# A list schedule whose due times come from its own latest times, from the first microsecond and in four passes

## The chip, the cores and the metric

The kernel runs on one core of a Trainium2 chip. The metric is the device time of one execution in microseconds (us). The engines named below are TensorE (PE, with its weight loads PEld), VectorE (DVE), ScalarE (ACT), GpSimd (POOL) and SyncE (SP), whose queue issues nearly all DMAs.

## What is computed

Attention over 4 batches of 8 heads, 768 positions and head size 64, in which a query sees the last 96 positions and the first 8 (with a linear penalty on the distance), followed by a dense layer of width 2048 with an ELU between its two products.

```python
scores = scale * np.matmul(q, k.transpose(0, 1, 3, 2))
scores = np.where(keep, scores + bias, -1000000000.0)
a = np.exp(scores - np.max(scores, axis=-1, keepdims=True))
x = (a / (np.sum(a, axis=-1, keepdims=True) + 1e-09)) @ v     # then heads side by side: (3072, 512)
h = x @ w_in                                                  # (512, 2048), stored as float64
g = np.where(h > 0.0, h, np.exp(np.minimum(h, 0.0)) - 1.0)
return g @ w_out                                              # (2048, 512), stored as float64
```

## The kernel before

The 3072 rows are cut into 12 groups of 256. The weights are cut into 16 chunks (fc 0 to 15) of each matrix. Every fp32 factor is split into a high and a low part, so a product takes three matmuls (high by high, high by low, low by high).

Groups 0 to 2 are computed plainly. Their attention works on pairs of heads (`pair32`, L677): scores on PE (L691), bias and maximum on DVE (L647), exponential on ACT (L649), the reciprocal of the sum on DVE (L662, L663), the scaling on ACT, DVE or POOL (L633, L635, L637), transposes (L708), their copies (tile `pt`), the product with v (L725), and the split of its result into tile `xh`. Their dense layer (`moe`, L737) runs fc 0 to 4 for the three groups, then fc 5 to 9, then 10 to 15: matmuls `h` (L803), the ELU (`elu`, L731: ACT, ACT, DVE), its split into `gh` and `gl`, and two steps later the matmuls `o` (L763). The pairs' loads share three buffers for `rqv` and three for `rk`.

The weights arrive as float64 bits. `weight` (L413) turns each of the 32 chunks into two fp32 parts: a load (L425), one ACT and four DVE operations (L433 to L442), a cast on ACT, a subtraction on POOL or DVE; 24 of the chunks are then stored again in DRAM (`kept`, L449). `combos` (L453) builds sums of second-layer weights, which groups 3 to 11 need: they compute the second product in seven block products instead of eight (`moe7`, L808, matmuls `a`, L877). Group 3's attention is still of the plain kind; those of groups 4 to 11 are woven between the matmuls in `visit` (L596).

No order of work is written by hand. `build` (L930) adds some thousands of operations to a `Plan`, each with the engines that can do it and a cost in ns for each, the tiles that it reads and writes, and a due time worked out by hand: d - 8000 for the ELU, d - 5500 to d - 2000 for a weight's steps, where d is the time at which the chunk's matmuls are meant to run; the start of group 3 plus 6.6 us for each chunk's `combos`; windows in `ATT` for attention. The hand-written start of group 3 is 178.8 us (30.0 + 16 x 3.5 + 32 x 2.9).

`order` (L147) is a list schedule. Of the operations that an engine could start next it takes one that can start now over one that must wait, and among those the one with the earliest due time. Tiles of one class are given buffers in the order in which they were added, whatever is due. An operation with several engines goes to the one that would finish it first, by where those engines stand, not by what is queued for them. PE operations of the late groups have a fixed sequence (`seq`).

`latest` (L115) goes backwards over a finished plan. PE gets an ideal line: from `since` on its operations in their planned sequence without gaps, and before `since` their planned starts. Every other operation gets the latest time by which it must start so that its consumers, and the next user of its buffer, keep theirs. That time becomes its due time:

```python
at = op.start if at is None or op.start < since else at      # L128, PE's ideal line
if op.seq is None and op.eng != "PE" and op.start > since:   # L141
    op.due = op.late
```

`run` (L1039) plans once by hand-written due times, then `PASSES` times takes latest times and plans again, and emits the last plan. Each engine executes its share in that order. Before emission the loads of chunks 2, 3 and 4 (`ASKED`) are moved to just behind the eleventh load of attention. `run` also puts eleven small operations for an input flag (L1093 to L1108) at a fixed number of places behind the last transposes.

Of the kernel before, what the change touches and what calls it, by code (L numbers as in the profile page):

```python
# [275 lines left out]
class Kernel:  # L276
# [732 lines left out]
    PERIOD, SECOND, DOWN, DOWN2, VISIT = 13200.0, 2890.0, 6730.0, 9250.0, 9245.0  # L1009
    OPENS = (0, 2, 6)  # L1010
    AFTER = 2 * PERIOD
    PASSES, SINCE = 2, 195000.0
    GS, KEEP, COMBO = 3, 100000.0, 0.0
    LATE, ASKED = 11, (2, 3, 4)
    ABS = (0, 1)
# [294 lines left out]
```

## Time and profile before

| | us |
|---|---|
| median of 3 runs | 657.53 (656.42 to 657.7) |
| the profiled execution | 657.34 |
| its span, first to last instruction | 655.6 |
| PE, DVE, ACT, POOL busy in the span | 641.5, 521.2, 478.2, 39.5 |

The difference of 1.74 us between the profiled execution's time and its span lies around the program. A matmul's end is modelled in the profile, so PE counts as busy through short waits; the wait of a weight load (PEld) for another engine is the sharper sign that PE had nothing to do.

### The profile page before, as it was taken

To read this page: it belongs to the slowest core of one execution; us is meant where nothing else is said; L and a number is where in the kernel's file an instruction comes from. 1 tells how busy PE (TensorE), PEld (TensorE's weight loads), DVE (VectorE), ACT (ScalarE), POOL (GpSimd) and SP (SyncE) were. 2 spreads that over 40 slices of the span, in tenths; PEclk is the share of its full clock that TensorE was granted. 3 is DMA by queue.
4 is the path that set the end of the run, shared out by engine and by line. 5 is a ranking of instruction groups with operands and counts; after the bars stand their busy time and mean duration, and the time that the engine had idled before them with its cause. 6 is when DMAs were issued, how large, how long until landed. Compare 5 with 4: busy or idle time off the path is not lost.

```text
span 655.6 us, 15992 instructions
## 1 busy us (share of the span) xinstructions
PE 641.5 (98%) x5950; PEld 598.6 (91%) x5950; DVE 521.2 (80%) x1509; ACT 478.2 (73%) x1243; POOL 39.5 (6%) x65
## 2 busy tenths in 40 slices
PE   8899999999999999999999999999999999999996
PEld 6677888888888999999999999999999999999995
DVE  7999999999998867866877886876777778765654
ACT  7998878766878776877777776786777867773542
POOL 4143001110211000000000000000000000000000
PEclk9999999999999999999999999999999999999999
DMA  7936996710237567667766747756775775674751
GB/s 272 307 112 216 389 339 257 264 65 12 77 113 261 185 215 254 221 202 243 241 196 211 267 174 235 250 205 221 227 242 186 248 257 180 210 250 140 248 171 38
DMA packets 52377, 137.75 MB, mean 210 GB/s; under 512 B 5698, under 2 KB 19010, under 8 KB 52290
## 3 DMA queue, kind: packets, MB, share of 16 engines
q1 hardware_dynamic: 52000, 136.37, 61.2%
q8 instruction: 49, 0.80, 0.5%
q10 hardware_dynamic: 290, 0.26, 0.1%
q14 instruction: 38, 0.31, 0.1%
HBM read 119.84 MB, written 16.78 MB: 208 GB/s over the span
## 4 chain that ended last, share of the span: by engine, by line
PE 82%; DVE 12%; ACT 3%; issue 1%; DMA 1%; POOL 0%; POOLq 0%; SPq 0%; DVEq 0%
PE h L803 35%; PE a L877 27%; PE o L763 6%; PE pv L614 4%; PE s L556 3%; PE t L576 3%; DVE g L464 2%; PE pv L725 1%; PE t L708 1%; ACT pr L649 1%; DVE gl L344 1%; DMA rqv<-in_qkv_dram 1%; DVE e L735 1%; PE s L691 1%; DVE g L440 1%
## 5 line engine op out<-in xcount | busy, mean ns | idle before, releaser
L803 PE MATMUL h<-xh,w0s 128*128 128x256 f32 x1728 | 203.1, 276 | 0.0
L803 PEld LDWEIGHTS h<-xh,w0s 128*128 128x128 f32 x1728 | 199.5, 188 | 0.1
L877 PE MATMUL a<-w,gg 128*128 128x256 f32 x864 | 143.7, 277 | 0.3 <-DVE xh L344 0.3
L336 ACT CAST gg<-z 128x384 fp32r<-128x384 f32 (+1 forms) x144 | 81.3, 565 | 70.4 <-DVE z L735 30.4
L735 DVE SCALAR_TENSOR_TENSOR z<-z,h 128x512 f32<-128x512 f32 x72 | 49.5, 688 | 95.2 <-ACT z L734 87.2
L877 PEld LDWEIGHTS a<-w,gg 128*128 128x128 f32 x864 | 120.4, 188 | 0.5 <-DVE xh L344 0.5
L649 ACT ACTIVATE pr<-pr,nmax 128x232 f32<-128x232 f32 (+1 forms) x192 | 90.0, 471 | 9.0 <-DVE nmax L647 8.6
L344 DVE TENSOR_TENSOR gg<-z,gg 128x512 fp32r<-128x512 f32 (+1 forms) x144 | 84.9, 618 | 7.4 <-ACT gg L336 6.6
L803 PEld LDWEIGHTS h<-xh,w 128*128 128x128 f32 x576 | 81.5, 189 | 8.8 <-issue 1.4
L803 PE MATMUL h<-xh,w 128*128 128x256 f32 x576 | 86.9, 283 | 0.0
L835 DVE TENSOR_TENSOR z<-z 128x128 f32<-128x128 f32 (+1 forms) x216 | 72.0, 333 | 5.2
L877 PE MATMUL a<-ta,gg 128*128 128x256 f32 x432 | 72.4, 276 | 0.0
L733 ACT ACTIVATE z<-h 128x512 f32<-128x512 f32 x72 | 43.0, 597 | 34.8 <-PE h L803 34.5
L647 DVE CUSTOM_DVE_ANT_0 pr<-s,tab 128x232 f32<-128x232 f32 (+1 forms) x192 | 63.4, 373 | 5.6 <-PE s L556 5.6
L763 PE MATMUL o<-w,gh 128*128 128x512 f32 x192 | 59.7, 403 | 1.7 <-DVE ob L790 1.2
L877 PEld LDWEIGHTS a<-ta,gg 128*128 128x128 f32 x432 | 59.7, 188 | 0.0
L877 PE MATMUL a<-tb,gg 128*128 128x256 f32 x216 | 50.0, 294 | 0.0
L734 ACT ACTIVATE z<-z 128x512 f32<-128x512 f32 x72 | 45.5, 631 | 1.8
L633 ACT ACTIVATE pr<-pr,st 128x232 f32<-128x232 f32 (+1 forms) x89 | 38.5, 468 | 9.7 <-DVE st L669 7.4
L763 PEld LDWEIGHTS o<-w,gh 128*128 128x128 f32 x192 | 32.0, 188 | 6.8 <-ACT pr L649 1.6
L877 PEld LDWEIGHTS a<-tb,gg 128*128 128x128 f32 x216 | 34.4, 188 | 3.8 <-issue 0.2
L649 ACT ACTIVATION_READ_ACCUMULATOR pr<-pr,nmax 128x1 f32 x192 | 36.8, 191 | 0.0
(128 smaller groups left out, 923.9 us busy)
## 6 DMA issues: line engine op xcount, KB each, us to landing
w0s<-kept SPq DMA_DIRECT2D x144, 512.0 KB, 5.0
rk<-in_qkv_dram SPq DMA_DIRECT2D x45, 184.0 KB, 2.7
bits<-in_w_in_dram SPq DMA_DIRECT2D x16, 512.0 KB, 6.3
bits<-in_w_out_dram SPq DMA_DIRECT2D x16, 512.0 KB, 9.3
kept<-w SPq DMA_DIRECT2D x16, 512.0 KB, 4.4
rv<-in_qkv_dram SPq DMA_DIRECT2D x32, 256.0 KB, 3.6
rqv<-in_qkv_dram SPq DMA_DIRECT2D x13, 384.0 KB, 3.5
rqv<-in_qkv_dram SPq DMA_DIRECT2D x34, 128.0 KB, 3.6
```

Source lines behind the costliest of these rows:

```text
L336: self.nc.scalar.copy(out, x)
L344: self.on(e).tensor_tensor(out, x, y, ALU.subtract)
L633: self.nc.scalar.activation(out, x, AF.Copy, scale=sc)
L647: p.add((("DVE", 158 + 1.042 * n, False),), lambda e: nc.vector.tensor_tensor_reduce(pr.t[:, lo:], st_()[:, lo:], tab, -(2.0 ** -(h + 1)), ...
L649: p.add(act(n, extra=200), lambda e: nc.scalar.activation(pr.t[:, lo:], pr.t[:, lo:], AF.Exp, bias=nm, scale=-1.0, accum_out=st.t[:, 0, i: ...
L733: p.add(act(n, True), lambda e: nc.scalar.activation(out(), hx(), AF.Relu, scale=-1.0), [h], [ex], due)
L734: p.add(act(n), lambda e: nc.scalar.activation(out(), out(), AF.Exp, scale=-1.0), [ex], [ex], due)
L735: p.add(dve(n), lambda e: nc.vector.scalar_tensor_tensor(out(), out(), -1.0, hx(), ALU.add, ALU.max), [h, ex], [ex], due)
L763: nc.tensor.matmul(acc[i].t, g.t[:, i * P:(i + 1) * P], w2.t[:, s], start=fc == f0 and n == 0 and s == HI, stop=fc == f1 - 1 and n == 1)
L803: self.nc.tensor.matmul(hx(), w1.t[:, s, cc * P:(cc + 1) * P], xh.t[:, x, cc], start=n == 0 and cc == 0, stop=n == 2 and cc == self.NCC - 1)
L835: tt = lambda e, out, x, y, op: self.on(e).tensor_tensor(out, x, y, op)
L877: nc.tensor.matmul(of[i].t[:, j], gg.t[:, x, g], w(s), start=first and x == s == 0 and n in (0, 2, 4, 6), stop=last and x == LO and n in ( ...
```

## The change

Two constants of the planner. `SINCE` becomes 0, so that all operations but PE's take their due times from latest times, and PE's ideal line has no gaps from its first operation on; before, that held for what was planned to start after 195 us. `PASSES` becomes 4, so the plan is made five times instead of three. PE's own operations keep the due times and sequence that they had. No operation is added or left out; what can change is the order on each engine, the engine of an operation that has a choice, and the buffer that a tile gets.

```diff
@@ -1009,7 +1009,7 @@
     PERIOD, SECOND, DOWN, DOWN2, VISIT = 13200.0, 2890.0, 6730.0, 9250.0, 9245.0
     OPENS = (0, 2, 6)
     AFTER = 2 * PERIOD
-    PASSES, SINCE = 2, 195000.0
+    PASSES, SINCE = 4, 0.0
     GS, KEEP, COMBO = 3, 100000.0, 0.0
     LATE, ASKED = 11, (2, 3, 4)
     ABS = (0, 1)
```

## Rows read from the trace of the kernel before

**Rows 1.** The profile's page: busy us, share of the span, instructions of each engine.
```profile
PE 641.5 (98%) x5950; PEld 598.6 (91%) x5950; DVE 521.2 (80%) x1509; ACT 478.2 (73%) x1243; POOL 39.5 (6%) x65
```

**Rows 2.** Busy time by stage: stretch, length, engines' busy us (instructions), clock, DMA share, GB/s.
```profile
10.00:60.00 50.00, 45.91 (x370) 35.19 (x371) 48.42 (x166) 45.61 (x145) 15.85 (x24) 1.00 0.62 206
60.00:70.00 10.00, 10.00 (x90) 8.64 (x89) 8.64 (x30) 9.67 (x30) 3.33 (x6) 1.00 1.00 383
70.00:140.00 70.00, 70.00 (x478) 61.32 (x477) 69.14 (x179) 57.24 (x148) 5.48 (x9) 1.00 0.74 274
140.00:200.00 60.00, 58.40 (x409) 50.12 (x408) 59.79 (x150) 41.88 (x119) 9.31 (x10) 1.00 0.24 78
200.00:590.00 390.00, 390.00 (x4049) 379.01 (x4048) 291.21 (x855) 292.22 (x743) 1.55 (x3) 1.00 0.67 224
590.00:606.00 16.00, 15.67 (x148) 15.17 (x148) 9.28 (x27) 6.50 (x12) 0.00 (x0) 1.00 0.41 144
```

**Rows 3.** The chain that ended last, 198 to 590 us, shares by line.
```profile
by line: PE h L803 43.5%; PE a L877 38.3%; PE pv L614 6.8%; PE s L556 5.7%; PE t L576 4.4%; PE o L763 1.1%; PE th L576 0.3%
```

**Rows 4.** The same chain, 590 to 606 us.
```profile
by line: PE h L803 38.3%; PE a L877 18.6%; DVE gg L344 13.3%; DVE z L835 5.9%; DVE z L735 4.3%; ACT z L734 4.0%; DVE xh L344 3.8%; ACT z L733 3.8%; DVE flag L1093 1.7%; issue 1.5%; DVE flag L1100 1.0%; DVE flag L1101 1.0%; DVE flag L1094 1.
```

**Rows 5.** The same chain, 3 to 76 us: shares, then pieces (start, us, what).
```profile
by line: PE o L763 11.8%; ACT pr L649 10.6%; PE pv L725 9.9%; DMA rqv<-in_qkv_dram 9.5%; PE h L803 9.3%; PE t L708 9.3%; PE s L691 6.6%; ACT pt L336 3.8%; issue 3.3%; POOL pr L637 2.8%; DVE gl L344 2.1%; DVE pr L647 2.0%; PE none L1078 1.9%
...
18.98 3.22 DMA rqv<-in_qkv_dram
...
28.86 0.57 ACT g L433
...
45.28 3.74 DMA rqv<-in_qkv_dram
...
54.60 0.60 DVE g L442
```

**Rows 6.** Who waited for whom, 5 to 70 us: total us, times, longest us.
```profile
POOL pr L637 <- DVE st L663: 19.8, 6, 5.4
...
PEld t L708 <- POOL pr L637: 2.7, 7, 0.7
PEld s L691 <- ACT rqv L633: 2.0, 2, 1.7
PEld t L708 <- ACT pt L336: 1.8, 2, 0.9
...
PEld s L691 <- DVE rqv L635: 1.0, 3, 0.6
...
PEld pv L725 <- ACT pr L649: 0.6, 2, 0.4
...
PEld s L691 <- DVE g L440: 0.2, 1, 0.2
```

**Rows 7.** The DMA queue's own waits, 5 to 70 us.
```profile
SPq L516 <- PE pv L725: 20.9, 9, 5.1
```

**Rows 8.** Who waited for whom, 70 to 200 us, PE and its weight loads.
```profile
PE o L763 <- DVE ob L790: 1.2, 1, 1.2
...
PEld o L763 <- ACT pr L649: 1.6, 1, 1.6
PEld o L763 <- ACT gh L336: 0.8, 2, 0.5
PEld o L763 <- DVE gl L344: 0.7, 3, 0.3
```

**Rows 9.** DVE by line, 70 to 140 us: count, busy us, mean ns, idle before.
```profile
L440 DVE SCALAR_TENSOR_TENSOR g<-bits,g 128x512 int32<-128x512 int32 x19 | 12.8, 679 | 0.0
...
L735 DVE SCALAR_TENSOR_TENSOR e<-e,h 128x256 f32<-128x256 f32 x22 | 8.9, 407 | 0.0
L344 DVE TENSOR_TENSOR gl<-e,gh 128x256 fp32r<-128x256 f32 x21 | 8.7, 415 | 0.5 <-ACT gh L336 0.5
```

**Rows 10.** The chain that ended last, 140 to 192 us, shares by line.
```profile
by line: DVE g L464 25.7%; DVE e L735 9.4%; DVE gl L344 8.6%; issue 8.0%; DVE ta L344 7.8%; DVE w L344 4.4%; DVE g L440 4.2%; DVE tb L344 3.6%; PE o L763 3.1%; DVE pr L647 2.9%; PE h L803 2.7%; DVE xh L344 2.7%; DVE ob L790 2.5%; DVE g L442
```

## The prediction

> **What bounds the kernel now.** I read the page first, then the busy time by stage, then the chain that ended last in each stage, and last the waits. The page says PE 98% busy [rows 1], but its busy time is modelled, so the stages matter more. From 200 to 590 us PE is busy without a break, its weight loads for 379.01 of 390 us, while DVE and ACT have 98.8 and 97.8 us to spare [rows 2]; the chain of that stretch is PE alone [rows 3]. There is nothing to win there. Before 200 us it is another kernel: DVE is busy for 48.42 of 50 us, then 8.64 of 10, 69.14 of 70 and 59.79 of 60 [rows 2], because it does attention for groups 0 to 3, the weights' conversion and the `combos`. ACT is nearly as full up to 70 us (45.61 of 50 and 9.67 of 10). From 3 to 76 us only 48.8% of the chain, 35.6 of 73 us, is PE (11.8 + 9.9 + 9.3 + 9.3 + 6.6 + 1.9) [rows 5]; the rest is ACT, DVE, POOL and two loads. So the reader should look for what PE lacks in the first 70 us, and then check that the change doesn't spoil what follows.
>
> What PE lacks there: its weight loads wait 2.7 us for scaled probabilities from POOL, 2.0 and 1.0 us for scaled queries, 1.8 us for copied transposes, and 1.7 us in five smaller rows, the first of 0.6 and the last of 0.2 us [rows 6]: 9.2 us in all. From 70 to 200 us it is 1.6 + 0.8 + 0.7 us and 1.2 us for the output copy `ob`, 4.3 us [rows 8]. These 13.5 us are all that any order of the work could win back before 200 us, and a part of it is owed to engines that are full, not to their order.
>
> **The change, part by part.**
>
> First, no instruction is added or removed. What moves is the order on DVE, ACT, POOL and SP for everything planned before 195 us: softmax, conversion, ELU, `combos`, loads, the `kept` stores. PE's operations keep hand-written due times, and classes of tiles keep their order, so pairs follow pairs and chunks follow chunks as before; what is free is how the streams are interleaved.
>
> Second, from 3 to 76 us. The chain runs through weight conversion that stands ahead of attention on its engine: pieces like 0.57 us of L433 on ACT at 28.86 and 0.60 us of L442 on DVE at 54.60 [rows 5]. POOL shows the same from its side: it sat idle for 19.8 us, six times, waiting for a DVE reciprocal (L663) [rows 6], a step that the plan costs at 0.29 us; its inputs, or it, had queued behind longer work. Hand-written due times can't know which buffer the next pair waits for; latest times do, since they follow the next user of a buffer too. So the short links of the attention chain should get ahead of conversion that PE needs later. What can come of it: the waits on POOL, on `pt` and on small rows (2.7 + 1.8 + 1.7 = 6.2 us) come from order and from capacity together; I take 40%, -2.5 us. The scaled queries (3.0 us) stand behind loads of 3.22 and 3.74 us on the chain [rows 5], which begin as soon as a buffer is free; those I leave. A bound from capacity: between 10 and 70 us DVE is idle for 1.58 + 1.36 = 2.94 us [rows 2]. Work conserved on DVE can't end earlier by more than that unless some of it goes to POOL, which has 40.8 of 60 us free, or to ACT with 4.7. So -2.94 us, and at the far end about -4.5 when a few operations change engine. On the other side, a wrong interleaving can add as much as it can save: +4.5.
>
> Third, from 70 to 200 us. PE is covered now: the ELU's due time of d - 8000 puts it ahead of conversion at d - 5500 and later, and the `o` matmuls come two steps of 2.9 us behind their `h`. The stalls that remain are 1.2 us on `ob`, which the buffer rule of the latest times should see coming, and 1.6 + 0.8 + 0.7 us [rows 8]. With latest times the ELU loses its fixed lead and gets just what the next `o` needs. I book -1.0 us for `ob` and +1.0 us for more stalls of the ELU, together 0; bounds -2 and +5 (the second rival). The `combos` fill a quarter of the chain between 140 and 192 us (25.7% for L464) [rows 10], although group 3's second product is the first to need them; in both kernels they are due last and run only where DVE is free, so they stay where they are, at 0.
>
> Fourth, SP. All loads and `kept` stores get new due times. SP is seldom the one that is late: its longest waits are for buffers (20.9 us in nine waits of L516 for L725 [rows 7]), and an order by need keeps those. Taken at 0; if a conversion load stood ahead of an attention load, the price is what DMA shows on the chain, 3.22 to 3.74 us [rows 5], once.
>
> Fifth, two more passes and a line without gaps. From 200 us on all latest times move earlier by about the same amount, so their order holds, and PE is full in its fixed sequence: 0. One piece can move: the flag's operations and ELU of the last group stand on the chain between 590 and 606 us, where PE's h and a make 56.9% [rows 4]; the flag's place counts operations, so it can slip off or stay: 0, between -1 and +1 us.
>
> Sum: -2.5 (second), 0 (third to fifth). Against the profiled execution's 657.34 us that is 654.8; the median of the runs, 657.53, lies 0.2 us above that execution, so I say 655.0 us, 0.4% faster.
>
> **The rivals.**
>
> Rival A, no change: capacity, not order. DVE and ACT are full where PE waits, so an earlier operation pushes another one back, and PE's own order, which doesn't change, hands the new due times the old interleaving. For it: 48.42 of 50 us on DVE [rows 2]. Against: POOL's 19.8 us behind a reciprocal [rows 6]. It gives 657.5 us, within 1.3 us.
>
> Rival B, slower: the ELU without its lead. From 70 to 140 us DVE has no idle time, and each of the ELU's two DVE steps (0.407 and 0.415 us) can stand behind a conversion step of 0.679 us that began just before [rows 9]. One such step ahead of each costs a chunk 1.4 us, which the 5.8 us between `h` and `o` absorb; three ahead of each (4.1 us) it no longer absorbs together with the chain's own five operations of about 0.4 us (2 us). From there every chunk can stall PE by some 0.3 to 0.7 us. 22 chunks lie between 70 and 140 us [rows 9] and, as an estimate at the same pace, 19 in the 60 us behind them; a quarter of these 41 at 0.45 us is 4.6 us: 662 us. For it: PE's weight loads already wait for gh and gl in five places [rows 8]. Against: the same planner works with latest times after 200 us without a stall; but there DVE is free for a quarter of the time.
>
> Rival C, buffers. Nine times SP waited for the `pv` matmul of an earlier pair before it could load the next queries, 20.9 us in total [rows 7], and the load then stood on the chain. If it is those three buffers that set the pace of attention up to 70 us, any order gives the same stalls, and the time is 657.5 us. The Trainium skill (Perfetto Trace Analysis, Identifying Performance Opportunities) says that the same gap repeated on the engine that should be saturated can mean that there isn't enough memory for the next tile. By that rule the repeated waits of the pairs would be a matter of buffers and my second part would be worth nothing.
>
> Rival D, the plan wanders: each pass plans on the order of the pass before, the last one is taken whether or not it is the best, and the model of the plan is not the chip. Where the first 70 us lose one more load of 3.22 to 3.74 us on the chain [rows 5], the time is 661 us.
>
> The change may also not do what it says where the interleaving is ruled by PE's due times and by the order of the classes; that is rival A.
>
> **How the numbers follow.** Forecast (about 655.0, own range 650.8 to 656.2): 0.43. Rival A 0.15 and rival C 0.10, both at 657.5: 0.25 for no change. Rival B 0.18, rival D 0.14: 0.32 for slower, 659 to 664. A difference of 0.2%, 1.3 us, is about what a measurement of this kernel can tell from no change. The low end is the far bound of the second part with that of the third, -4.5 and -2, 650.8; the high end takes in rival B's 662. Less than 2 in 10 lies outside.
>
> **What would show it.** Right: in the chain from 3 to 76 us fewer pieces of conversion (L433 to L442) and a share of PE above 48.8%; the weight loads' waits for POOL and `pt` below 4.5 us together; group 3's first matmuls `h` of the woven kind some 2 us earlier; from there to the end the same length. Rival A: the same waits in other places. Rival B: waits of `o` for gh and gl between 70 and 200 us well above 1.5 us. Rival C: SP's waits for `pv` near 20.9 us and the attention of group 2 ending where it ended. Rival D: more than two loads of `rqv` on the chain. I am wrong altogether if the stretch after 200 us changes length by over 1 us.

## The result

The changed kernel takes 664.38 us (median of six runs, 663.13 to 665.23) against 657.62 us for the kernel before, measured beside it. The ratio is 1.0091, with a 95% interval of 1.0072 to 1.0109: 0.9% slower, where 0.4% faster was forecast. The profiled execution took 665.16 us, its span is 663.4 us.

The profile's page of the kernel before has these two lines for the matmuls of groups 3 to 11, the first product `h` and one part of the second, `a`:

```profile
L803 PE MATMUL h<-xh,w0s 128*128 128x256 f32 x1728 | 203.1, 276 | 0.0
...
L877 PE MATMUL a<-w,gg 128*128 128x256 f32 x864 | 143.7, 277 | 0.3 <-DVE xh L344 0.3
```

The page of the changed kernel shows more time for the same counts, 4.6 us for `h` and 1.5 us for `a`, of the 8.0 us by which PE's busy time has grown:

```profile
PE 649.5 (98%) x5941; PEld 606.0 (91%) x5941; DVE 519.1 (78%) x1503; ACT 479.9 (72%) x1248; POOL 43.9 (7%) x66
...
L803 PE MATMUL h<-xh,w0s 128*128 128x256 f32 x1728 | 207.7, 279 | 0.0
...
L877 PE MATMUL a<-w,gg 128*128 128x256 f32 x864 | 145.2, 278 | 0.3 <-DVE xh L344 0.3
```

The busy time by stage of the changed kernel, columns as in [rows 2]:

```profile
10.00:60.00 50.00, 45.91 (x362) 34.77 (x362) 46.59 (x159) 45.80 (x146) 14.20 (x23) 0.97 0.56 189
...
70.00:140.00 70.00, 70.00 (x478) 61.22 (x477) 69.38 (x176) 57.05 (x151) 7.82 (x8) 1.00 0.78 294
140.00:200.00 60.00, 59.53 (x417) 51.57 (x417) 59.03 (x154) 43.85 (x123) 15.43 (x16) 1.00 0.24 75
200.00:590.00 390.00, 390.00 (x3985) 379.21 (x3984) 287.34 (x846) 288.06 (x735) 0.78 (x2) 1.00 0.66 220
```

The reader should look at the last line beside that of [rows 2]. PE is full in both, its weight loads are busy for 379 us in both, the clock is 1.00 in both; but in the same 390 us the changed kernel executes 3985 matmuls where the kernel before executed 4049. In this stretch PE waits for nobody, and yet less gets done: its matmuls follow each other more slowly. The stages before 200 us, in which the order of the work changed most, end almost level. (The 9 matmuls fewer on the page, 5941 for 5950, lie there: they are filler matmuls, whose number follows the gaps of the plan, 24 for 22 at L1078 and none for 11 at L1087.) The first woven `h` matmul starts at 202.09 us, before at 201.84 us. From there to the end of the span it is 461.3 us instead of 453.7: 7.6 us, all of the loss.

The chain that ended last shows where. A piece `h x48` is four chunks' worth of matmuls that stream one buffer of tile `xh`. In the kernel before, pieces between 238 and 292 us (start, us, what):

```profile
239.52 5.44 PE h L803 x48
253.16 5.44 PE h L803 x48
264.90 5.44 PE h L803 x48
278.54 5.44 PE h L803 x48
```

In the changed kernel:

```profile
240.05 5.44 PE h L803 x48
253.75 5.74 PE h L803 x48
265.89 5.74 PE h L803 x48
279.91 5.74 PE h L803 x48
```

The first piece belongs to group 3, the others to group 4. Group 3 runs at the old pace, group 4 at 5.74 us, and so it alternates to the end: every second group is slow. Groups alternate between two buffers for `xh`, xh0 and xh1. The slow ones are those on xh1.

So I took the buffer of every PE operation from the two plans and measured in the two traces how far apart the starts of successive matmuls of one operation lie on average (256 columns each; the moving data is streamed through PE, the stationary data is what the weight load puts there):

| matmuls | before | after |
|---|---|---|
| h, moving data in xh0 (960 woven matmuls) | 113.7 ns | 113.9 ns |
| h, moving data in xh1 (768 woven matmuls) | 113.9 ns | 119.6 ns |
| a, stationary data in gg0, moving data in tile `ta` (202 spacings) | 113.7 ns | 117.3 ns |
| a, stationary data in gg1, moving data in `ta` (196) | 113.7 ns | 113.4 ns |
| a, last group, stationary data in xh1 (51) | 113.4 ns | 118.4 ns |
| a, all with stationary data in gg0 (555, some pairs with gaps in both) | 121.0 ns | 123.6 ns |

The built programs say what happened to these buffers. A pool gives addresses in the order in which buffers are first used. In the kernel before, the planned first use of xh1 (group 1's attention result) stood 0.6 us ahead of that of gg0 (the first `gh`). In the changed kernel it stands 0.3 us behind. The two changed places in SBUF, the memory from which PE reads them, and as they differ in size their addresses moved:

| buffer | start before, bytes | by 256 | start after, bytes | by 256 |
|---|---|---|---|---|
| xh0 | 175008 | 160 | 175008 | 160 |
| xh1 | 184736 | 160 | 192224 | 224 |
| gg0 | 193248 | 224 | 184928 | 96 |
| gg1 | 201440 | 224 | 201440 | 224 |
| w012 to w015, the ring of h's weights | 38112, 42208, 8928, 4832 | 224 | the same | 224 |

The constants `PLACE`, with their odd offsets of 32, 48, 80 and 160 words, put these remainders there; they hold only for the order of first use that the old plan gave.

### The profile page after: what moved, and what is told of

It is laid out like the page before. It is cut to its first block, busy times and chain, and to the rows that moved or that the text cites. A ratio compares the mean times of both kernels' runs of the same rounds, so it can differ in the third digit from the quotient of the medians.

```text
span 663.4 us, 15966 instructions
## 1 busy us (share of the span) xinstructions
PE 649.5 (98%) x5941; PEld 606.0 (91%) x5941; DVE 519.1 (78%) x1503; ACT 479.9 (72%) x1248; POOL 43.9 (7%) x66
## 4 chain that ended last, share of the span: by engine, by line
PE 88%; DVE 6%; ACT 2%; issue 1%; DMA 1%; POOL 0%; SPq 0%; POOLq 0%; ACTq 0%
PE h L803 38%; PE a L877 27%; PE o L763 9%; PE pv L614 4%; PE s L556 3%; PE t L576 3%; PE pv L725 1%; PE s L691 1%; PE t L708 1%; DMA bits<-in_w_in_dram 1%; DVE g L440 1%; ACT pr L649 1%; DVE g L442 1%; DVE w L344 0%; DVE g L438 0%
## 5 line engine op out<-in xcount | busy, mean ns | idle before, releaser
L803 PE MATMUL h<-xh,w0s 128*128 128x256 f32 x1728 | 207.7, 279 | 0.0
L803 PEld LDWEIGHTS h<-xh,w0s 128*128 128x128 f32 x1728 | 204.1, 189 | 0.1
L877 PE MATMUL a<-w,gg 128*128 128x256 f32 x864 | 145.2, 278 | 0.3 <-DVE xh L344 0.3
L633 ACT ACTIVATE pr<-pr,st 128x232 f32<-128x232 f32 (+1 forms) x95 | 40.3, 467 | 9.3 <-DVE st L669 7.7
L734 ACT ACTIVATE z<-z 128x512 f32<-128x512 f32 x72 | 45.5, 633 | 1.8
```

The costliest lines, as they stand in the source:

```text
L633: self.nc.scalar.activation(out, x, AF.Copy, scale=sc)
L734: p.add(act(n), lambda e: nc.scalar.activation(out(), out(), AF.Exp, scale=-1.0), [ex], [ex], due)
L803: self.nc.tensor.matmul(hx(), w1.t[:, s, cc * P:(cc + 1) * P], xh.t[:, x, cc], start=n == 0 and cc == 0, stop=n == 2 and cc == self.NCC - 1)
L877: nc.tensor.matmul(of[i].t[:, j], gg.t[:, x, g], w(s), start=first and x == s == 0 and n in (0, 2, 4, 6), stop=last and x == LO and n in ( ...
```

## The experiments

Two theories stood against each other. P: the loss is placement, that is, addresses. S: it is the schedule, in the way of rivals B and D. The first two runs are a cross of the two orders with the two sets of addresses. To hold the addresses, every buffer is touched once in a fixed order before any work; no instruction comes of it.

**Order of the changed kernel, addresses of the kernel before.**

```diff
+    LAYOUT = "w015 w014 w115 w114 ... st5 e1 xh1 gg0 gl0 gg1 gl1 gh2 gl2 qs0 ks0 part0 part1 vd0"
...
         with self.tc.manual_schedule():
+            for s in self.LAYOUT.split():
+                (self.w if s[0] == "w" else self.m).tile([P, self.LINE], F32, tag=s, name=self.n("at"))
             self.setup()
```

> The changed kernel's order of work, but every buffer is given the address that it has in the kernel before (the buffers are touched once, in the old order, before any work). Theory P (placement): the 7 us are lost after 200 us because two buffers, xh1 and gg0, changed places in SBUF, and matmuls that read them take 120 and 117.5 ns instead of 114; with the old addresses h on xh1 is back at 114 ns and the time is 657.6 us, within 1.5. Theory S (schedule: the ELU without its lead, or a wandering plan): the time stays at 664, since the order is that of the changed kernel.

Measured: 657.96 us, a ratio of 0.9997 (0.9988 to 1.0006) to the kernel before. h on xh1 takes 113.9 ns, and the pieces of the chain are back:

```profile
253.21 5.44 PE h L803 x48
264.95 5.44 PE h L803 x48
278.59 5.44 PE h L803 x48
```

The loss is gone although the order on all engines is that of the changed kernel. S falls.

**Order of the kernel before, addresses of the changed kernel.** The same lines, with gg0 ahead of xh1 and the other pairs swapped as the changed kernel has them.

> The order of the kernel before with the addresses of the changed kernel. Theory P: slower by 768 matmuls x 6.1 ns (h on xh1) + 555 x 3.5 ns (a with gg0) + 51 x 5 ns, 6.9 us, so 664.5 us; the first woven h stays at 201.8 us. Theory S: 657.6 us.

Measured: 664.36 us, 1.0097 (1.0081 to 1.0112). h on xh1 takes 119.6 ns, and the chain has the slow pieces:

```profile
252.26 5.74 PE h L803 x48
264.39 5.74 PE h L803 x48
278.42 5.74 PE h L803 x48
```

The addresses alone make the whole loss, on a program whose order wasn't touched. The sum expected was 6.9 us; the medians differ by 6.2.

**SINCE = 0 with two passes, addresses held.**

```diff
-    PASSES, SINCE = 4, 0.0
+    PASSES, SINCE = 2, 0.0
```

> SINCE = 0 with two passes as before, addresses of the kernel before. Theory P: 657.6 us within 1.5, like the changed order on the old addresses. Theory S: near 664, if the due times are to blame and not the further passes. The plan's own end is 0.4 us later than before's, so a schedule effect alone should be under 1 us.

Measured: 655.99 us, 0.9968 (0.9956 to 0.9980). Faster than the kernel before by 2.2 us, more than the bound of 1.5 that I had set. So the new due times can gain something, but not in the plan that four passes arrive at.

**Four passes with SINCE = 195000, addresses held.**

> Four passes with SINCE = 195000, addresses of the kernel before. 50 places of the order differ from the kernel before, and the plan ends at the same time. Both theories: 657.6 us within 1; a change of more would mean that the later groups' order matters by itself.

Measured: 658.38 us, 0.9998 (0.9985 to 1.0011): nothing, as both expected. Two further passes over the late groups only change nothing.

**Which addresses cost.** Four runs of the kernel before, in which xh0 and xh1 are moved inside their room by changing `PLACE` alone, for instance

```diff
-             ... "xh0": (160, 0), "xh1": (32, 0), "gg0": (80, 0), ...
+             ... "xh0": (128, 32), "xh1": (96, 0), "gg0": (16, 0), ...
```

> The kernel before with its two buffers of moving data shifted by some bytes inside their room; everything else stays in place. A start's remainder by 512 bytes was 416 for xh0 and xh1 and 224 for all four weight buffers of the ring; in the changed kernel xh1 had 224. Here xh1 has 160 and xh0 288. If equal remainders are what costs (theory E), both groups of h stay at 114 ns; if only 416 is good (theory G), both go to 120 ns.

> The same with remainders 96 (xh1) and 352 (xh0). Theory E: 114 and 114 ns. Theory G: 120 and 120 ns, about 9.4 us longer in all. A third, that the distance to 224 counts in steps of 64 bytes: between the two.

> The same with remainders 32 (xh1) and 480 (xh0). Theory E: 114 and 114 ns. Theory G: 120 and 120 ns.

> The same with remainders 192 (xh1) and 256 (xh0), 32 bytes to either side of the weights' 224. Theory E with a grain of 64 bytes or more: at least one of the two at 120 ns; with a grain of 32 bytes: both at 114 ns. Theory G: both at 120 ns.

Measured, one run each beside 657.76 us: 662.69, 667.98, 667.54 and 663.84 us. By buffer, the woven h (median over the operations of four matmuls each; the ring's weights stay at 224 by 256):

| start of the moving data by 512 | by 256 | ns |
|---|---|---|
| 160 and 416 | 160 | 113.3 and 113.3 |
| 32 and 288 | 32 | 117.7 and 117.7 |
| 96 and 352 | 96 | 117.3 to 120.3 in both, 118.9 and 119.1 on average |
| 224 and 480 | 224 | 120.0 and 120.0 (the 224 from the changed kernel) |
| 192 | 192 | 117.0 to 119.0 |
| 256 | 0 | 117.0 |

Starts that lie 256 bytes apart give the same spacing, in all four pairs; so for the moving data the address counts by its remainder by 256, as far as these pairs go. Theory E (only equal remainders cost) falls: five of six remainders cost something, equality costs most. G is nearer the truth once it is read by 256, with 160 the only one of the six that costs nothing, though it set all costs at 120 ns. The starts of xh in the kernel before were not neutral ground but the best of the six remainders tried: a move to any other of them loses.

**Is it the distance to the weights?** Three of the ring's four buffers are moved, xh stays.

```diff
-    PLACE = {"w015": (80, 0), "w014": (0, 48), "w012": (80, 0), "w013": (0, 48), ...
+    PLACE = {"w015": (80, 0), "w014": (16, 32), "w012": (64, 16), "w013": (32, 16), ...
```

> The kernel before, with three of the ring's four weight buffers shifted inside their room and the buffers of moving data left at a remainder of 160 by 256. The weights' remainders by 256 are now 160 (w012), 96 (w013), 32 (w014) and still 224 (w015). If the distance from weights to moving data counts (theory R, relative), the woven h take 120 ns on w012 (distance 0), 117.7 on w013 (64), 118.9 on w014 (128) and 113.3 on w015 (192, as before), by the figures of the runs that moved xh. If only the moving data's own address counts (theory A), all four stay at 113.3 ns.

Measured: 661.38 us, one run beside 657.81. By weight buffer, the same on xh0 and xh1: w012 119.7 to 120.0 ns, w013 113.3, w014 115.3 to 120.7, w015 113.3 to 113.7. Theory A falls, since the moving data stood still. R is right for three buffers and wrong for w013: there the weights start at 96 and the moving data at 160, and the spacing is 113.3 ns; with weights at 224 and moving data at 32, the same distance by 256, it was 117.7. So the weights' start counts beside that of the moving data, but the distance alone isn't the rule. Nor do the two remainders settle it. The `a` matmuls of the changed kernel on gg0 have weights at 96 and moving data at 160 too, and take 117.3 ns. And in the run with xh0 at 288, the last group's `a` with weights in xh1 took 117.6 ns instead of 113.4, though their own two operands lay where they lie in the kernel before. What the rule is stays open, and so does the part of the matmul in which it acts.

**The changed due times with other numbers of passes, addresses left to themselves.** `PASSES` of 2, 3 and 1, and nothing held:

> SINCE = 0 with two passes and nothing else touched. In this order xh1 is first used before gg0, so the two keep the addresses of the kernel before; three smaller buffers (gh2, gl2, qs0) change places. Theory P: 656.0 us within 1, as with all addresses held. Theory S, were it still alive: 664.

Measured: 655.54 us, 0.9971 (0.9958 to 0.9984): 2.3 us faster than the kernel before, as with the addresses held. These two are the best kernels of the study. This one differs from the kernel before in `SINCE` alone.

> SINCE = 0 with three passes and nothing else touched. Here the order touches gg0 before xh1, as in the changed kernel, so both have the changed kernel's addresses. Theory P: 663 to 665 us. If it is the fourth pass that costs: 656 to 658.

Measured: 665.03 us, 1.0107 (1.0083 to 1.0130), with h on xh1 at 119.6 ns. It is not the fourth pass: three passes are already slow, because the plan puts gg0 first, and by no more than 0.07 us of planned time.

> SINCE = 0 with one pass and nothing else touched; xh1 and gg0 as in the kernel before. Theory P: 655.5 to 658.5 us. The plan's own end is 0.9 us later than with two passes; if that counted on the chip, 657.

Measured: 663.93 us, 1.0101 (1.0075 to 1.0127), far outside the range that I expected. And here it is not placement: h takes 113.7 and 113.9 ns, and from the first woven h to the end of the span it is 453.9 us, as before. But that first h starts at 207.84 us, 6.0 us late. The chain between 14 and 40 us, of which four pieces (start, us, what):

```profile
18.76 1.89 DMA rk<-in_qkv_dram
...
22.74 2.02 POOL pr L637 x4
24.77 0.04 issue
24.81 1.54 PE t L708 x6
```

PE's transposes waited for a load and then for POOL, which scaled four pieces of probabilities one after another. With the same addresses of xh1 and gg0 as two passes have, one pass loses 6.1 us before 200 us. A part of it can be the clock, which was granted at 0.83 on average between 20 and 30 us of this execution; as an estimate, that costs at most 1.7 us if PE was busy throughout. So a schedule can lose as much as the placement did; it just didn't in the changed kernel.

## Why the prediction was wrong

The range of 650.8 to 662.0 us did not hold 664.38, and the sign was wrong. By its own steps:

**What bounds the kernel now** was read rightly as to where PE waits: between 200 and 590 us it waits for nothing in [rows 2] and [rows 3]. "There is nothing to win there" stands, as no run won anything there; the silent second half, that there was nothing to lose either, was wrong. A PE that is always busy has one more thing that can change, the pace of its matmuls, and the profile's rows gave it: pieces of 5.44 us for 48 matmuls are 113.3 ns each.

**The fifth part** is the step that failed: "From 200 us on all latest times move earlier by about the same amount, so their order holds, and PE is full in its fixed sequence: 0." PE did stay full. The addresses of its operands didn't hold, and 0 should have been what the pace costs: as an estimate from the table of spacings, 768 x 5.7 ns for h on xh1 is 4.4 us, 735 x 2.6 ns for all a on gg0 is 1.9 us, and 63 x 5.0 ns for the last group's a on xh1 is 0.3 us, 6.6 us in all. The medians differ by 6.8 us; of the 7.6 us by which the stretch grew in the two profiled executions, 1.0 us is not accounted for. The text ahead of the prediction says that the buffer that a tile gets can change, and `PLACE` stands in the code with offsets that serve no computation. I priced order, engine and waits, and never asked what the offsets are for. The prediction's own last sentence, that I was wrong altogether if the stretch after 200 us changed length by over 1 us, is what came true: 7.6 us.

**The first part** isn't quite right: the nine filler matmuls fewer are a change in the program. It doesn't touch the cause, since the run with the order of the changed kernel and the old addresses has the same fillers as the changed kernel.

**The second part** forecast -2.5 us between 3 and 76 us. Two passes gained 2.2 us (addresses held) and 2.3 us (left alone), but not there, so the likeness of the numbers is luck. The last weight load for group 2's `pv` starts at 75.6 us in the kernel before, at 75.7 and 75.2 us with two passes, and with four at 76.9 (addresses held) and 78.0 us (the changed kernel). The sign that I had named, PE's share of the chain, comes out all the same in one of the two runs. The chain from 3 to 76 us with two passes and addresses left alone:

```profile
by line: PE o L763 13.9%; PE h L803 13.6%; PE pv L725 12.1%; PE t L708 11.3%; DMA rqv<-in_qkv_dram 9.0%; DMA bits<-in_w_in_dram 8.3%; PE s L691 8.1%; PE none L1078 3.1%; issue 2.8%; DVE g L442 1.7%; DVE g L440 1.6%; DVE pr L647 1.6%; ACT pr
```

and with the addresses held:

```profile
by line: DMA rqv<-in_qkv_dram 12.2%; PE pv L725 10.7%; PE o L763 9.2%; DMA bits<-in_w_in_dram 8.6%; PE t L708 8.3%; PE h L803 7.4%; PE s L691 6.8%; ACT pr L649 4.4%; issue 4.2%; PE none L1081 3.1%; POOL rqv L637 2.9%; ACT pt L336 2.1%; POOL
```

PE's lines make 62.1% of the first (13.9 + 13.6 + 12.1 + 11.3 + 8.1 + 3.1) and 45.5% of the second, where [rows 5] gave 48.8%; yet the two kernels are equally fast. So the share says along which line the chain was followed, not how fast the stage was. The other sign failed: pieces of conversion (L433 to L442) stand on the chain nine times in either run, seven times before. The same view of the changed kernel shows less PE, and a weight load at its head, as with two passes:

```profile
by line: PE h L803 8.3%; PE o L763 8.2%; PE s L691 8.1%; DMA bits<-in_w_in_dram 7.9%; PE pv L725 7.2%; PE t L708 7.0%; issue 6.0%; ACT pr L649 5.2%; DVE g L440 4.6%; POOL pr L637 4.1%; ACT pt L336 3.2%; DVE pr L647 3.1%; DVE g L442 3.0%; DV
...
3.55 5.80 DMA bits<-in_w_in_dram
```

On the chip one pass costs 6.1 us, two gain 2.2 us, four gain 0.2 us with the addresses held, inside the interval of no change. That each pass gives another plan is rival D's mechanism, at 0.14; it named only a loss of one load.

**The third part** had the right wait and the wrong sum. It booked -1.0 us for `ob` and +1.0 us for the ELU. PE's waits for the ELU between 70 and 200 us in the changed kernel, beside 0.8 and 0.7 us in [rows 8]:

```profile
PEld o L763 <- ACT gh L336: 0.9, 3, 0.4
...
PEld h L803 <- DVE e L735: 0.7, 2, 0.5
...
PEld o L763 <- DVE gl L344: 0.3, 1, 0.3
```

Those of `o` are 1.2 us, before 1.5; that of `h` grew from 0.3 to 0.7. So the +1.0 us didn't come, and the wait for `ob` is gone. It was one stall of the kernel before, and the prediction counted it twice, as PE's 1.2 us and as 1.6 us of a weight load:

```profile
189.11 0.30 PEld L763 LDWEIGHTS o<-w,gh 128*128 128x128 f32 x2 [1.64 <-ACT pr L649]
...
189.14 0.70 PE L763 MATMUL o<-w,gh 128*128 128x512 f32 x2 [1.23 <-DVE ob L790]
```

Here the two-pass kernels drew ahead: their first woven h starts at 199.86 us (addresses left alone) and 200.33 us (held), before at 201.84. Up to 180 us they and the kernel before have executed 238 `o` matmuls each; from 180 to 190 us, before and with two passes (addresses left alone):

```profile
180.00:190.00 10.00, 8.77 (x62) 7.36 (x62) 9.96 (x26) 7.03 (x22) 2.56 (x2) 1.00 0.03 10
...
180.00:190.00 10.00, 10.00 (x71) 8.74 (x70) 9.96 (x31) 8.03 (x25) 2.51 (x2) 1.00 0.15 43
```

With four passes the stall is gone too, but 235 `o` matmuls (addresses held) are done by 180 us: in these traces an early loss and this gain cancel, and the order is worth nothing (0.9997). How much of the 2.2 us is this stall isn't shown: it is missing as well in three of the six other traces with the order of the kernel before, those with the addresses of the changed kernel, with xh at 192 and 256, and with the ring moved.

Rival B, at 662 us the nearest to the result, was near it for a reason that isn't there: with the addresses held the same order runs in 657.96 us.

**The fourth part** took SP at 0. In the changed kernel the conversion step on ACT (L433) that waits for the weight load of 5.80 us starts at 9.43 us, before at 8.65, and the first `pv` matmul at 12.2 us, before at 11.4. By 200 us this no longer shows: the first woven h comes 0.25 us later than before.

**Rival C**, buffers: SP's waits for the `pv` matmuls, in the kernel with two passes, beside 20.9 us in [rows 7]:

```profile
SPq L516 <- PE pv L725: 25.5, 9, 5.3
```

They grew by 4.6 us, and group 2's attention ended 0.4 us earlier, 0.1 us later with the addresses held. That the attention ends where it ended is what rival C expects, and rival A too; the gain came behind, where neither had looked. The rule of the Trainium skill (Perfetto Trace Analysis, Identifying Performance Opportunities), by which a repeated gap can mean that memory for the next tile is short, speaks of the engine that should be saturated. Here the waits are SP's, and no run changed the number of buffers, so whether these buffers set the pace of the early stage is not shown.

## What to carry to other kernels

Where a planner or an allocator decides buffers, a change of order can be a change of addresses too: before pricing an edit at nothing in a stretch where PE is full, ask which buffers its matmuls read and whether they stay in place. Count matmuls per stretch, not only busy time: 3985 against 4049 in the same 390 us at the same clock is a slower pace, and no wait showed it. To learn what an order is worth, hold the addresses; in this kernel that separated an order worth nothing from a loss of 6 us. And where a gain has the forecast size, look whether it arose in the forecast place.

## What the runs showed of the hardware

The pace of the 128 x 256 fp32r matmuls of this kernel changed with where operands start in SBUF: 113.3 ns at the best starts, 117.0 to 120.3 ns at most others, up to 6% in a stretch that PE fills. Starts of the moving data that differ by 256 bytes gave the same pace in all four pairs tried. Both operands' starts matter: moving the weights alone took the pace from 113.3 to 120 ns. The worst case found, three times, is moving data and weights at the same remainder by 256. A matmul's own two starts are not the whole of it, as the 117.6 ns for unmoved operands show.

In the early stage the granted clock can fall, and it did in the profiled execution of the changed kernel. Two lines of its busy time by stage, columns as in [rows 2], the clock third from the end:

```profile
22.00:26.00 4.00, 2.12 (x10) 1.46 (x10) 3.87 (x17) 3.07 (x11) 0.80 (x2) 0.92 0.97 353
26.00:30.00 4.00, 4.00 (x26) 2.73 (x25) 3.04 (x13) 2.55 (x9) 0.74 (x2) 0.65 1.01 399
```

PE had been busy for 2.12 of the first 4 us; in the next 4 us the granted clock was 0.65 on average, so for most of them at the lower of its two levels, 1.2 of 2.4 GHz. With the addresses held the same order kept PE busy for 2.11 us of the first stretch, and the clock was 1.00 in both. In these two executions the last weight load for group 2's `pv` starts at 78.0 us with the fall and at 76.9 us without, and the first woven h at 202.09 and 201.89 us; so little of the fall is left there. It has no part in the loss between 200 and 590 us, where the clock is 1.00 in both kernels.
